# First loads in another order, an early exp at the change of layers, eps on VectorE for single tiles, and new places for the DVE units

## The chip, the cores and the metric

The kernel runs on one core of a Trainium2 chip. The core has five engines with instruction queues of their own: PE (TensorE, matrix products), ACT (ScalarE, activation functions), DVE (VectorE), POOL (GpSimd) and SP, which issues the transfers here. They meet through semaphores. Matrix products write to PSUM, eight banks of 128 x 512 floats. The metric is the device time of one launch in microseconds; the median of three runs of the kernel before is 1564.82 us (1563.92 to 1565.23).

## The reference, cut to what matters

Two pairs of layers, each an attention with one shared key and value head and then a gated MLP that mixes along the sequence; 2,048 positions, width 512, 32 heads of 16, hidden width 896 in each half:

```python
def attention(x, wq, wk, wv, wo):       # 32 query heads, one k and one v for all
    q = (x @ wq).reshape(B, S, H, Dh).transpose(0, 2, 1, 3)
    k, v = x @ wk, x @ wv
    p = softmax(einsum('bhqd,bkd->bhqk', q, k) * Dh ** -0.5)
    return einsum('bhqk,bkd->bhqd', p, v).transpose(0, 2, 1, 3).reshape(B, S, H * Dh) @ wo

def gmlp(x, w_in, w_sp, b_sp, w_out):
    z = gelu(x @ w_in)                  # tanh form
    z1, z2 = z[..., :Fh], layernorm(z[..., Fh:])
    g = einsum('ts,bsf->btf', w_sp, z2) + b_sp[None, :, None]
    return (z1 * g) @ w_out

for _ in range(2):
    x = x + attention(layernorm(x), wq, wk, wv, wo)
    x = x + gmlp(layernorm(x), w_in, w_sp, b_sp, w_out)
```

## The kernel before, in words

The program is a list of operations (`op`, `dma`, `dve`) with the tiles that they read and write, a planned duration and a priority. `_Graph.op` derives the dependencies from the keys of those tiles: an operation waits for the last writer of what it reads, and for the last writer and all readers since of what it writes. `schedule` plays the list through with planned durations and puts every engine's operations into an order by hand, as it were: whichever is ready and has the lowest priority number goes next. Where PE has too little to do, it puts in filler products (`warm`, `add_zeros`, lines 737 to 751). `emit` writes the five queues in that order, each operation with its semaphore waits. So a changed place, duration or priority can move any later instruction.

Attention is computed in groups: 32 a layer, each of 512 query columns (for the usual chunk of two tiles of 128 positions, two query columns of 256 side by side), against 16 key tiles. A unit is one group against one key tile: four blocks of 128 x 512 scores (line 925). A unit goes one of two ways.

- On ACT (`push_unit`, `push_slot`): blocks are taken two or three at a time into a slot of PSUM banks, and one activation (line 950) makes the exp of all of them and writes it to `P_ring`; then PE multiplies with V (line 969). Slots alternate between three blocks (banks 0 to 2) and two (banks 3 and 4). In a group whose bit is set in `NARROW`, both kinds have two, and bank 2 is left to side products. The planner counts 0.051 + 0.4267 us a block for an exp.
- On DVE (`push_unit_dve`): the exp is approximated with integer additions on the bits of bfloat16: four instructions of 128 x 512 (line 1003), two of 128 x 2048 (line 1012), and three PV products in place of one (line 1018).

`ON_DVE` lists for each layer and group the key tiles that go to DVE. All other work, which is called side work here, is laid between these: layer norms, keys, values, queries, the front of the MLP (`b_front`), the mixing along the sequence (`mix_stage`, `mix_late`) and the output products.

At the start, `load_x` and `load` (line 764) issue the first transfers from SP's queue, in this order: tiles 0 and 1 of X, wk, wv, wq, tiles 2 and 3 of X, then the rest. The layer norms of the first four tiles are made singly (`per_tile`): statistics on DVE (817, 818), eps added on POOL (805), the power -0.5 on POOL (807), the normalization on DVE (823), the transposition on PE (838).

At the change of layers, when the last exp of layer 0 is done, `gelu_rest` applies gelu to the rest of z2 (1272) and to z1 (1284); the last front tile brings its own gelus (1209, 1236). Then `mix_late(0, 0, ...)`, which the program lists with layer 1, adds up the mixed sums of the first two tiles (`sums_lead`, 1451), multiplies z1 by them (1459; for later tiles 1419), makes the output products (718, `w_out_r<-`), adds to X (1114), and the norms, keys and queries of layer 1 follow. The first query tile goes through ACT (`qT`, 891), and then layer 1's exps start. ACT needs another table for exp than for gelu; the table loads (ACT_TABLE_LOAD) are put in by the compiler ahead of the first activation that needs one.

After the last exp of layer 1 comes the tail: `gelu_rest` again, and `mix_late(1, ...)` for all four column blocks.

Of the kernel before, what the change touches and what calls it, by code (L numbers as in the profile page):

```python
# [8 lines left out]
I16 = mybir.dt.int16  # L9
ACTF = mybir.ActivationFunctionType  # L10
# [10 lines left out]
NF1 = 7  # L21
# [31 lines left out]
), (  # L53
# [29 lines left out]
NARROW = (4194528, 10506244)  # L83
KEEP = 6
POOL_ON = 1
POOL_XN = 0
# [42 lines left out]
class _Op:  # L129
    __slots__ = ("eng", "fn", "dur", "lat", "prio", "seq", "deps", "succ", "nleft", "chan", "chan_val",  # L130
                 "inc", "pos", "val", "clock", "t0", "task", "mode", "rows", "work", "opens", "nstart", "due", "chain", "free_lat",
                 "empties", "near_end", "heads")

    def __init__(self, eng, fn, dur, lat, prio, seq, chan, task, mode):
# [6 lines left out]
        self.heads = None  # L141
        self.opens = None
# [22 lines left out]
class _Graph:  # L165
# [3 lines left out]
    def __init__(self, nc, side, slots):  # L169
# [10 lines left out]
        self.chain = False  # L180
        self.nsem = 0
# [13 lines left out]
    def op(self, eng, fn, dur, r=(), w=(), prio=5, lat=0.0, chan=None, mode=0):  # L195
        task = next((x for x in (*w, *r) if isinstance(x, _Task)), None)
        o = _Op(eng, fn, dur, lat, prio, len(self.ops), chan, task, mode)
        o.chain = self.chain
# [34 lines left out]
    def schedule(self):  # L233
# [31 lines left out]
        slot_due = -1.0  # L265

# [73 lines left out]
        def pick(e):  # L340
# [7 lines left out]
            for ent in ready[e]:  # L348
# [6 lines left out]
                if beside(o):  # L355
                    p -= 2.0
                if best is not None and (p, o.seq) >= best[:2]:
                    continue
# [63 lines left out]
        while True:  # L422
            moved = True
            while moved:
                moved = False
                for e in ENGS:
                    if free[e]:
# [12 lines left out]
                        us = o.dur  # L440
                        if e == "pe":
# [126 lines left out]
def bass_interleave_layers__grouped_kv_mqa__mixer_gmlp__prompt_kernel(  # L568
# [43 lines left out]
    mhalf = G.sb([P, 1], FP32, "mhalf")  # L612
    mone = G.sb([P, CT], FP32, "mone")
    X = G.sb([P, NT, D], BF16, "X")
# [40 lines left out]
    ph16 = big[:].bitcast(I16)  # L655
    wspL = big[:, 4:6, :].rearrange("p a (t q) -> p a t q", q=QC)
# [72 lines left out]
    op("pool", lambda e: e.memset(mone[:], -1.0), 0.1, w=["mone"])  # L729
    op("pool", lambda e: e.memset(zeros[:], 0.0), 0.2, w=["zeros"])  # L730
# [29 lines left out]
    def load(dst, src, w, chan, kb, r=()):  # L760

        first["kb"] += kb
        first["n"] += 1
        dma(lambda e: e.dma_start(dst, src), list(r), w, chan, max(3.0, 3.2 + first["kb"] / 380.0 - 0.6 * first["n"]))

    def load_x(t0, n):
        load(X[:, t0:t0 + n, :], xsrc[:, t0:t0 + n, :], [("X", t) for t in range(t0, t0 + n)], f"x{t0}", 128 * n)
# [712 lines left out]
    for layer in range(2):  # L1480
        now["layer"] = layer
        now["group"] = 0
        for t0, n in KEYS[layer]:
# [7 lines left out]
            for si in range(NQ):  # L1491
                if sum(GROUPS[2 * si][:2]) == t0 + n:
                    q_slot(si, pr + (0.3 if si else 0.1) if layer else 3)
# [45 lines left out]
```

## Time and profile before

| | us |
|---|---|
| median of three runs (lowest to highest) | 1564.82 (1563.92 to 1565.23) |
| the profiled execution, its own time | 1566.62 |
| its span, first to last instruction | 1564.7 |
| PE busy | 1492.9 (95%) |
| ACT busy | 1484.2 (95%) |
| DVE busy | 1379.3 (88%) |
| POOL busy | 330.3 (21%) |
| exps (L950): 1289 instructions, busy | 1416.7 |
| DVE units, scores part (L1003): 980 instructions, busy | 645.0 |
| transfers, mean | 66 GB/s |

Busy time of an engine is the time in which at least one of its instructions runs; PE's contains fillers, and its products overlap. In a row of a group, the count stands behind the x, then busy microseconds and the mean nanoseconds of one; behind the second bar stands the idle time just before these instructions and what ended it. Exps overlap one another by some 0.2 us, so the mean of one is longer than the step from one to the next. A row of the timeline gives start, duration, engine, line, operation, what it writes and reads, and in brackets the idle time before it.

### The profile page before, as it was taken

The numbers are of one execution on the slowest core, as the hardware profiler recorded it, in microseconds if no ns is written. First come the engines' busy times: TensorE is split into PE (matmuls) and PEld (weight loads), VectorE is DVE, ScalarE is ACT, GpSimd is POOL, SyncE is SP. The second block draws the span as 40 slices with busy tenths as digits, with TensorE's granted clock in tenths as the row PEclk, the third lists the DMA queues.
The fourth block names the chain that finished last, engine by engine and source line by source line (L and its number), as shares of the span: only waits on it lengthen the run. The fifth ranks groups of instructions, "written<-read, shape, count | busy, mean of one in ns | idle before, by whom it ended". The sixth has DMA issues, their size and how long they took to land.

```text
span 1564.7 us, 40919 instructions
## 1 busy us (share of the span) xinstructions
PE 1492.9 (95%) x18024; PEld 487.1 (31%) x18054; DVE 1379.3 (88%) x2368; ACT 1484.2 (95%) x1336; POOL 330.3 (21%) x319
## 2 busy tenths in 40 slices
PE   8999999999999999999999999999999999999999
PEld 3222222233333233333422222323223322323343
DVE  7989999999999888886778899999899998888887
ACT  6999999999999999999799999999999999999970
POOL 2031121212221112111210025212122211212232
PEclk9999999999999999999999999999999999999999
DMA  4501010101212433545431031110121023155472
GB/s 103 136 15 15 8 26 9 22 16 39 52 35 42 98 77 116 149 109 151 114 88 21 8 78 29 21 15 15 38 59 29 22 71 90 42 153 150 109 202 68
DMA packets 186833, 103.21 MB, mean 66 GB/s; under 512 B 151072, under 2 KB 159904, under 8 KB 186656
## 3 DMA queue, kind: packets, MB, share of 16 engines
q1 hardware_dynamic: 186656, 100.60, 25.8%
q8 instruction: 141, 2.31, 0.6%
q14 instruction: 36, 0.29, 0.1%
HBM read 34.77 MB, written 29.88 MB: 41 GB/s over the span
## 4 chain that ended last, share of the span: by engine, by line
ACT 69%; PE 24%; DVE 5%; issue 1%; DMA 1%; POOL 0%; SPq 0%; DVEq 0%
ACT P_ring L950 67%; PE ps_all L713 8%; PE ps_all L925 7%; PE ps_all L969 3%; PE ps_all L718 3%; PE ps_all L1018 3%; ACT z2n L1249 1%; DVE big L1414 1%; DVE big L1003 1%; DVE X L1114 0%; DVE st L1293 0%; DVE st L817 0%; ACT L950 0%; ACT L1249 0%; DMA X<-in_A_x_dram 0%
## 5 line engine op out<-in xcount | busy, mean ns | idle before, releaser
L950 ACT ACTIVATE P_ring<-ps_all 128x1024 bf16<-128x1024 f32 (+1 forms) x1289 | 1416.7, 1313 | 18.6 <-PE ps_all L925 17.8
L1003 DVE TENSOR_SCALAR big<-ps_all 128x512 int16<-128x512 f32 x980 | 645.0, 684 | 88.9 <-PE ps_all L925 82.8
L925 PE MATMUL ps_all<-qT,kT_rep 32*128 32x512 bf16 x4096 | 602.5, 385 | 50.2 <-ACT P_ring L950 37.2
L1048 POOL TENSOR_TENSOR rden<-ot,mone 128x16 f32<-128x16 bf16 x62 | 188.0, 3033 | 776.2 <-DMA ot<-oT 775.9
L925 PEld LDWEIGHTS ps_all<-qT,kT_rep 32*128 32x128 bf16 x4096 | 154.0, 91 | 569.4 <-ACT P_ring L950 468.3
L1012 DVE TENSOR_SCALAR big<-big 128x2048 int16<-128x2048 int16 x490 | 326.5, 687 | 3.5 <-PE ps_all L1018 0.7
L969 PE MATMUL ps_all<-P_ring,V_aug 128*32 128x512 bf16 x3116 | 296.1, 387 | 3.5 <-DVE oT L1091 2.6
L1018 PE MATMUL ps_all<-big,V_ph 128*32 128x512 bf16 x2940 | 258.7, 384 | 1.2 <-DVE big L1003 0.4
L969 PEld LDWEIGHTS ps_all<-P_ring,V_aug 128*32 128x32 bf16 x3116 | 75.8, 94 | 150.8 <-issue 122.2
L1018 PEld LDWEIGHTS ps_all<-big,V_ph 128*32 128x32 bf16 x2940 | 68.5, 94 | 97.9 <-issue 59.1
L805 POOL TENSOR_SCALAR ve<-mv 128x1 f32<-128x1 f32 (+2 forms) x44 | 16.1, 365 | 377.8 <-DVE mv L818 258.7
L713 PE MATMUL ps_all<-xnTA,z2n 128*32 128x512 bf16 x1344 | 94.8, 381 | 0.0
L713 PE MATMUL ps_all<-w_in_r,xo 128*32 128x448 bf16 x960 | 62.0, 354 | 0.2 <-DVE big L1003 0.2
L1114 DVE TENSOR_TENSOR X<-ps_all,X 128x512 bf16<-128x512 f32 x64 | 43.6, 683 | 19.1 <-PE ps_all L718 15.7
L713 PE MATMUL ps_all<-xo,w_in_r 128*32 128x256 bf16 (+1 forms) x1120 | 56.5, 317 | 0.1
L718 PE MATMUL ps_all<-w_out_r,z1c 128*128 128x512 bf16 x211 | 53.5, 381 | 2.1 <-issue 0.8
L1061 POOL TENSOR_TENSOR o_norm<-ot,rden 128x128 bf16<-128x128 bf16 (+1 forms) x118 | 53.3, 471 | 4.7
L751 PE MATMUL ps_all<-ones,zeros 128*32 128x512 bf16 x632 | 54.3, 385 | 0.0
L1350 DVE TENSOR_TENSOR big<-ps_all,big 128x512 f32<-128x512 f32 x56 | 38.2, 683 | 16.5 <-PE ps_all L713 16.1
L713 PE MATMUL ps_all<-z2n 128*32 128x512 bf16 x672 | 50.0, 382 | 0.0
L713 PE MATMUL ps_all<-z1c,z2n 128*32 128x512 bf16 x672 | 49.2, 382 | 0.0
L1419 POOL TENSOR_TENSOR z1c<-big,z1c 128x512 bf16<-128x512 f32 (+1 forms) x32 | 35.0, 1104 | 63.4 <-DVE big L1414 63.3
(99 smaller groups left out, 950.0 us busy)
## 6 DMA issues: line engine op xcount, KB each, us to landing
gp_scratch<-big SPq DMA_DIRECT2D x106, 256.0 KB, 2.1
big<-gp_scratch SPq DMA_DIRECT2D x99, 256.0 KB, 3.2
out_dram<-X SPq DMA_DIRECT2D x16, 128.0 KB, 1.7
w_in_r<-in_B_w_in_dram SPq DMA_DIRECT2D x1, 1792.0 KB, 7.9
big<-gp_scratch SPq DMA_DIRECT2D x14, 128.0 KB, 2.5
X<-in_A_x_dram SPq DMA_DIRECT2D x3, 512.0 KB, 6.5
bsp<-in_B_b_sp_dram SPq DMA_DIRECT2D x8, 128.0 KB, 3.7
ot<-oT SPq DMA_TRANSPOSE x62, 2.4
```

The source lines that it names most:

```text
L713: ins = e.matmul(out_[32 * j:32 * j + 32, :], lhs[:, 32 * j:32 * j + 32], rhs, tile_position=(0, 32 * j), start=start, stop=stop)
L718: return e.matmul(out_, lhs, rhs, start=start, stop=stop)
L751: ins = e.matmul(bank32(PVB)[32 * j:32 * j + 32, :], zeros[:, 0:32], mv, tile_position=(0, 32 * j), start=False, stop=False)
L925: return e.matmul(out, kT_rep[32 * j:32 * j + 32, a, u[1] * P:(u[1] + 1) * P], qT[32 * j:32 * j + 32, q, :], tile_position=(32 * j, 0), st ...
L950: return e.activation(P_ring[:, s0:s0 + n, :], bank32(b0, n).rearrange("p (k q) -> p k q", k=n), ACTF.Exp, scale=E_SCALE)
L969: ins = e.matmul(bank32(PVB)[32 * j:32 * j + 32, :], V_aug[:, kt, :], P_ring[:, s, :], tile_position=(0, 32 * j), start=first, stop=last)
L1003: o = dve(lambda e, box=box, tk=tk: e.tensor_scalar(ph16[:, tiles[0], heads["of"][box[0]] * QC:(heads["of"][box[0]] + 1) * QC], bank32(tk. ...
L1012: dve(lambda e, a=a: e.tensor_scalar(ph16[:, tiles[a], :], ph16[:, tiles[0], :], float(PH_A[a]), None, op0=ALU.add), 0.69, base, BIG(tiles ...
L1018: ins = e.matmul(bank32(PVB)[32 * j:32 * j + 32, :], V_ph[:, a, kt, :], big[:, tiles[a], j * QC:(j + 1) * QC], tile_position=(0, 32 * j), ...
L1048: op("pool", lambda e: e.tensor_tensor(rden[:], src()[:, :, :, DH], mone[:, :, None].to_broadcast([P, CT, 4]), ALU.pow), 3.0, r=[tk, "mone ...
L1061: op("pool", lambda e, b0=b0, nb=nb, dst=dst: e.tensor_tensor(dst, src()[:, b0:b0 + nb, :, 0:DH], rden[:, b0:b0 + nb, :, None].to_broadcas ...
L1114: dve(lambda e: e.tensor_tensor(X[:, t, :], bank32(tk.bank), X[:, t, :], ALU.add), 0.69, [tk, ("X", t)], [("X", t)], prio)
```

## The change

- `ON_DVE` is replaced: in layer 0 every group keeps its number of key tiles and gets other ones; in layer 1 both change. `NARROW` of layer 1 goes from groups 2, 12, 14, 21, 23 to groups 10, 11, 15.
- The first loads: tiles 2 and 3 of X are issued behind wk, ahead of wv and wq. The planner gets fixed durations for them, and 0.5 in place of 0.7 us for issuing.
- `rstd` adds eps on DVE where it works tile by tile, and as before on POOL elsewhere.
- `gelu_rest` in layer 0 ends with an exp of a 128 x 1 tile into `early`; it is listed as a reader of all z1 tiles.
- The w_out products of `mix_late` in layer 0 are marked `calm`: their later parts keep their own priority and don't get 1.0.
- New code that the constants leave unused: key tiles whose additions go to POOL (`ON_POOL` is empty, `port`, `step2`; one memset of `step2` on POOL runs), and a raised priority for the first tiles (`LEAD` is 0).

```diff
 ON_DVE = ((
-          (6,10,14), (6,10,14), (6,10,14), (6,10,14), (2,6,9,12,14), (2,3,12,13,14), (2,4,6,11,13),
...
+          (6,10,14), (6,10,14), (6,10,14), (6,10,14), (2,3,9,10,14), (4,5,9,13,14), (2,3,10,11,14),
...
 ), (
-          (6,10,14), (6,10,14), (10,14), (14,), (6,10,14), (6,10,14), (6,10,14), (2,10,14), (2,7,8,11),
-          (6,8,10,12,14), (3,6,9,12), (3,5,8,9), (2,7,11,12,14), (2,3,9,11), (4,6,9,12), (2,4,11,12),
-          (5,6,9,13), (4,6,8,9,14), (2,5,10,12), (2,7,8,10,14), (2,4,7,14), (4,8,10,11), (3,4,6,10,14),
-          (6,9,12,14), (2,6,14), (2,3,12,13,14), (6,), (2,4,6,12,14), (6,8,13), (2,9,12), (3,10,11,13),
-          (3,8,12)
+          (6,14), (6,10,14), (10,14), (14,), (6,10,14), (2,10,14), (6,10,14), (2,6,10,14), (2,3,9,11,12),
+          (2,3,4,11), (3,6,9,11,14), (3,6,9,11,14), (2,9,11,14), (2,3,6,10,11), (3,6,12), (3,6,9,11,14),
+          (4,9,11,14), (2,4,8,12,13), (3,6,10,11), (3,7,11,14), (2,3,7,13), (4,9,11,12,13), (3,5,7,11),
+          (3,7,8,9,14), (6,10), (2,3,10,13), (5,10,13), (2,6,12,14), (3,6,11,13), (4,9,12), (5,10,11,13),
+          (9,11,12)
 ))
...
-NARROW = (4194528, 10506244)
+NARROW = (4194528, 35840)
...
+    op("pool", lambda e: e.memset(step2[:], (PH_A[2] - PH_A[1]) * 65537), 0.1, w=["step2"])
...
-    load_x(0, 2)
-    load(wk_nat[:], A_wk.rearrange("(kd p) r -> p kd r", p=P), ["wk_nat"], "wk", 16)
-    load(wv_nat[:], A_wv.rearrange("(kd p) r -> p kd r", p=P), ["wv"], "wv", 16)
-    load(wq_r[:], A_wq.rearrange("(kd p) n -> p kd n", p=P), ["wq"], "wq", 512)
-    load_x(2, 2)
+    load_x(0, 2, 2.9)
+    load(wk_nat[:], A_wk.rearrange("(kd p) r -> p kd r", p=P), ["wk_nat"], "wk", 16, 3.0)
+    load_x(2, 2, 4.0)
+    load(wv_nat[:], A_wv.rearrange("(kd p) r -> p kd r", p=P), ["wv"], "wv", 16, 4.0)
+    load(wq_r[:], A_wq.rearrange("(kd p) n -> p kd n", p=P), ["wq"], "wq", 512, 5.0)
...
         for a, b in ([(i, i + 1) for i in range(i0, i0 + ni)] if per_tile else [(i0, i0 + ni)]):
-            op("pool", lambda e, a=a, b=b: e.tensor_scalar(ve[:, a:b], mv[:, a:b, 1], LN_EPS, None, op0=ALU.add),
-               0.25, r=[("mv" + n, i) for i in range(a, b)], w=[("ve" + n, i) for i in range(a, b)], prio=prio)
+            if per_tile:
+                dve(lambda e, a=a, b=b: e.tensor_scalar(ve[:, a:b], mv[:, a:b, 1], LN_EPS, None, op0=ALU.add), 0.15,
+                    [("mv" + n, i) for i in range(a, b)], [("ve" + n, i) for i in range(a, b)], prio)
+            else:
+                op("pool", lambda e, a=a, b=b: e.tensor_scalar(ve[:, a:b], mv[:, a:b, 1], LN_EPS, None, op0=ALU.add),
+                   0.25, r=[("mv" + n, i) for i in range(a, b)], w=[("ve" + n, i) for i in range(a, b)], prio=prio)
...
+        allk = []
         for t0, n in Z1_LATE:
             k = [("z1", f, t) for f in range(NF1) for t in range(t0, t0 + n)]
...
+            allk += k
+        if not now["layer"]:
+            op("act", lambda e: e.activation(early[:], mhalf[:], ACTF.Exp), 1.5, r=allk + [("z1", f, NT - 1) for f in range(NF1)] + ["mhalf"],
+               w=["early"], prio=5)
...
         for t in range(t0, t0 + n):
-            tk = _Task()
+            tk = _Task(calm=layer == 0 and CALM)
             products(tk, NF1, lambda e, ft, t=t, tk=tk: mm1(
                 e, bank32(tk.bank), z1c[:, ft, t * P:(t + 1) * P], w_out_r[:, ft, :], ft == 0, ft == NF1 - 1),
                 lambda ft: [("z1", ft, t), "w_out"], chain)
```

More of the change, by code (lines that the diff above doesn't have):

```diff
@@ L141, in __init__ @@
         self.heads = None
+        self.port = 0
         self.opens = None
@@ L180, in __init__ @@
         self.chain = False
+        self.lead = False
         self.nsem = 0
@@ L197, in op @@
         o = _Op(eng, fn, dur, lat, prio, len(self.ops), chan, task, mode)
-        o.chain = self.chain
+        o.chain = self.chain or self.lead
         if task is not None:
@@ L356, in pick @@
                     p -= 2.0
+                if o.port == 1 and now < long_till:
+                    p += PORT_LATE
+                if o.port == 2 and quick_till > now:
+                    continue
                 if best is not None and (p, o.seq) >= best[:2]:
@@ L440, in schedule @@
                         us = o.dur
+                        if o.port == 2:
+                            long_till = now + us
+                        elif o.port:
+                            if now < long_till:
+                                us += min(2 * (long_till - now) / 3, 1.2)
+                            quick_till = now + us
                         if e == "pe":
@@ L989, in push_unit_dve @@
         hg, kt, first, last = u[:4]
+        on_pool = ON_POOL[now["layer"]] and kt in ON_POOL[now["layer"]][now["gi"]]
         assert not first and not last
@@ L1456, in lead @@
                    prio=pr, lat=PE_LAT)
[L1457 to L1460 removed]
+            parts = [(t, t + 1) for t in range(n)] if LEAD > 1 else [(0, n)]
+            for a, b in parts:
+                z = z1c[:, f0:f0 + nf, a * P:b * P]
+                zk = [("z1", ft, t) for ft in fs for t in range(a, b)]
+                dve(lambda e, z=z, a=a, b=b: e.tensor_tensor(
+                    z, all_sums().rearrange("p (a q) -> p a q", q=w)[:, :, a * P:b * P], z, ALU.mult),
+                    0.15 + 0.135 * nf * (b - a), [tk] + zk, zk, chain + 0.01 * a)
         for f0 in range(0, NF1, m):
```

45 lines of the change are left out of this document (29 added, 16 removed), and 8 rows, old and new, of the table ON_DVE.

## The prediction

> **What bounds the kernel now.** I read the page's busy table first, then the waits of ACT, then busy time by stretch, and last the timeline around the two places where ACT stands still. The groups (with forms kept apart) and the waits of ScalarE:
>
> ```profile
> L950 ACT ACTIVATE P_ring<-ps_all 128x1536 bf16<-128x1536 f32 x538 | 837.6, 1557 | 6.1 <-PE ps_all L925 5.7
> L950 ACT ACTIVATE P_ring<-ps_all 128x1024 bf16<-128x1024 f32 x751 | 807.8, 1138 | 12.5 <-PE ps_all L925 12.1
> ```
> ```profile
> ACT P_ring L950 <- PE ps_all L925: 17.8, 11, 11.9
> ACT qT L891 <- PE ps_all L718: 9.7, 1, 9.7
> ```
>
> The second number of a wait is how often, the third the longest. One exp wait is the 11.9 us before the first exp, one wait is the 9.7 us at the change of layers; the other ten exp waits are 5.9 us together in 1,480 us. So ACT's exp stream sets the time: a start of 13.9 us, layer 0, the change, layer 1 to 1,496.7, then a tail of 68.0 us that PE and DVE share. A microsecond of exp work or of either standstill is a microsecond of the end. The stretches (columns: PE, weight load, DVE, ACT, POOL, granted clock, DMA share, GB/s) show how close the others are:
>
> ```profile
> 0.00:14.00 14.00, 10.45 (x113) 5.61 (x113) 9.88 (x29) 1.40 (x2) 6.97 (x27) 1.00 0.65 191
> 14.00:24.00 10.00, 9.43 (x116) 3.66 (x112) 7.83 (x20) 8.26 (x8) 1.28 (x2) 0.66 0.03 7
> 900.00:1100.00 200.00, 186.63 (x2382) 58.45 (x2379) 186.47 (x316) 199.08 (x180) 57.12 (x46) 0.99 0.16 31
> 1100.00:1300.00 200.00, 194.84 (x2382) 58.30 (x2379) 185.97 (x311) 199.70 (x188) 40.02 (x33) 1.00 0.17 44
> 1497.00:1565.00 68.00, 63.24 (x416) 28.09 (x410) 54.30 (x88) 17.33 (x16) 24.09 (x26) 1.00 0.46 132
> ```
>
> ACT is at 99.7% from 900 to 1300, but DVE there is already at 93%: 27.6 us idle in 400. The timeline at the start and at the change:
>
> ```profile
> 2.83 2.16 SPq L764 DMA_DIRECT2D X<-in_A_x_dram  x4
> 3.45 1.29 DVE L817 BATCH_NORM_STATS2 st<-X 128x6 f32<-128x512 bf16 x2 [0.62 <-DMA X<-in_A_x_dram]
> ...
> 7.41 0.69 DVE L817 BATCH_NORM_STATS2 st<-X 128x6 f32<-128x512 bf16 x1 [1.18 <-DMA X<-in_A_x_dram]
> 8.02 0.40 DVE L823 TENSOR_SCALAR xn<-X,mv,rs 128x512 bf16<-128x512 bf16 x1
> ```
> ```profile
> 746.20 2.53 ACT L1284 ACTIVATE z1c<-z1c 128x1792 bf16<-128x1792 bf16 x2
> 746.76 2.22 DVE L1459 TENSOR_TENSOR z1c<-ps_all,z1c 128x512 bf16<-128x512 f32 x4 [0.49 <-PE ps_all L1451]
> 749.26 2.97 PE L718 MATMUL ps_all<-w_out_r,z1c 128*128 128x512 bf16 x13
> 758.43 0.60 ACT L891 ACTIVATE qT<-ps_all 128x512 bf16<-128x512 f32 x1 [9.70 <-PE ps_all L718]
> 759.04 1.28 ACT L950 ACT_TABLE_LOAD   x1
> 760.34 10.60 ACT L950 ACTIVATE P_ring<-ps_all 128x1024 bf16<-128x1024 f32 x10
> ```
>
> At the start, DVE waits 1.18 us for the third tile of X while the finished statistics of the second wait behind it. At the change, the last gelu ends at 748.73, and the products z1*g (L1459), which the chain runs through, begin 2 us before that.
>
> **The change part by part.**
>
> *New places.* Layer 0 keeps its number of DVE units in every group, so its exp work is unchanged. Layer 1 goes from 117 to 119 units (two more, both among groups 8 to 21; groups 22 to 31 keep 36) and from five narrow groups to three. Stepping through the slot rule gives 714 two-block and 560 three-block exps for 751 and 538: 8 blocks and 15 instructions fewer. The kernel prices an exp at 0.051 + 0.4267 per block; all 1289 exps and 3116 blocks come to 1395 by that, against 1416.7 us on the page with the stalls in it, so it is close. Then -15 x 0.051 - 8 x 0.4267 = -4.2 us. With the difference of the two rows (0.419 a block) and the whole rest of 1416.7 spread over the instructions (0.086 each) it is -4.6. I take -4.2, since stalls need not fall with the count. For this DVE gets 2 x (4 x 0.684 + 2 x 0.687) = 8.2 us more, from the rows of L1003 and L1012, inside the 27.6 us idle; without that cover it would be +8.2 on the path. PE gets eight more PV matmuls a unit and more single score matmuls, some 2 us, hidden by its waits for ACT (14 to 17 us in every 50). What the other places do to the small stalls I can't read: I take 0. The stalls are 21 us in all (1416.7 - 1395), so a gain above some 4 is unlikely; and 4 lost would be four more like the longest exp wait in mid-stream, 1.28 us at 552.
>
> *First loads.* X's tiles 2 and 3 leave the queue third instead of fifth, at about 1.74 instead of 2.83. Alone in the queue X's first load took 2.7 us to its first use, so the third tile is there near 4.5 to 5, ahead of DVE. The wait of 1.18 goes; the second xn moves from 8.02 to about 6.6, and its transposes, kT and the first exp with it: -1.4. wv and wq are issued 0.5 us later; wq took 4.4 us to land, so about 7.2 to 7.8 with 256 KB now ahead of it, and its matmuls, at 10.52 before, would come near 9.1: still covered, with little over a microsecond. What is late next is DVE, which does statistics and kT in one queue. Ends: 0, if DVE's order eats it, and -2.5, if kT also no longer waits behind the statistics at 10.16.
>
> *The early exp.* It reads every z1 tile, and it is put into the program ahead of the layer-1 products that overwrite z1. So the dependency tracker makes each of them wait for it. L1459 then waits for: last gelu 748.73, table load 1.29, a 128x1 exp (the 128x384 and 128x512 activations took 0.48 and 0.60, which leaves about 0.15 to 0.2 for one element), the semaphore: about 750.25 instead of 746.76, +3.5. Behind L1459 in DVE's queue stand X's addition and the statistics of layer 1's first tiles, and PE waits for it with w_out (749.26, 0.28 after L1459's last), so the whole chain to qT moves by that. Back comes the load at 759.04: without it exp starts when the first scores are there, 759.38 plus 0.43 (the step from 13.45 to 13.88 at the start), 759.8 for 760.34: -0.5. The row of the wait gives the bounds: 0 if the products were late anyway, +3.6 if nothing overlaps.
>
> A page of the Trainium skill weighs on this. "ScalarE: Activation LUTs", section "What ACT_TABLE_LOAD costs", puts a switch of sets at about 2.66 us, load plus drain. Here the load at 730.10 is followed by a gelu at 731.39, 1.29 later, so this trace does not bear it out; so it gets no chance of its own. By the page the step would cost 1.4 more and the sum would be 1562.3.
>
> *eps on VectorE.* For single tiles 20 POOL instructions (128x1, 248 ns mean) become DVE ones. POOL's way from statistics to power is 0.40 us (752.39 to 752.79); on DVE a small instruction takes between 0.06 (the 128x1 memset) and 0.17 (aggregate), then a hop of 0.1. Saved: 0.1 to 0.25 each, where it lies on a chain: in the last front tile, whose gelus end ACT's run (-0.3, since that POOL eps took 0.39), at layer 1's second tile (-0.25), once in the tail (-0.2); at the start it is within the -1.4. DVE's 20 instructions are at most 3.4 us over the span, beside other work.
>
> *The rest at nothing.* One POOL memset of 0.10 us ahead of the ones delays only the first warming matmuls. The port, lead and POOL-unit code is switched off by its constants. The w_out products of layer 0 lose their raised priority once begun: an order between 761 and 900, where ACT waits little; within +-0.5. There the late start also lets the mixing work run ahead, and the gaps at 773, 899, 939 and 942 (0.49, 0.34, 0.51, 0.29) may shrink: -0.5.
>
> Sum: -4.2 - 1.4 + 3.5 - 0.5 - 0.3 - 0.25 - 0.2 - 0.5 = -3.9 (rounded). The span was 1564.7, and the profiled execution took 1566.62, 1.9 around the span and 1.8 above the median of the three runs, 1564.82. I take the difference off the median: 1560.9.
>
> **The rivals.** *More is gained.* The products' wait for the early exp costs nothing, because the products come later in the new order, or the stalls fall by as much: -3.9 - 3.5 = -7.4, 1557.4. Against it: L1459 follows its sums by 0.1 us and ACT is busy from 731 to 748.7 almost without a gap.
>
> *Two small gains fail.* DVE's order eats the earlier load and the gaps after 761 stay: -3.9 + 1.9 = -2.0, 1562.8, no measurable change. For it: between 10.2 and 13.4 DVE has no idle time before qT.
>
> *Slower: DVE becomes the bound between 900 and 1300.* It is at 93% and takes 8.2 us more in a stretch that should be 4.2 shorter: 380.6 of 396, 96%. If its idle 27.6 us is all waits for PE that no order removes, the stretch grows by 8.2 instead of shrinking by 4.2: 12.4 worse, 1573.3. It decides from 7 us lost, that is when more than half of the added DVE work shows. Against it: ACT does not wait for DVE units itself, only through PE's order and banks, and the listed exp waits on DVE are none.
>
> *The clock.* From 14 to 24 us the granted clock is 0.66 on average, and the first eight exps, 13.88 to 23.4, take about 2 us more than at full pace. "TensorE: Matmul & The Clock Gate" in the Trainium skill says the window that decides this is free-running (section "What's actually happening"); three runs cannot show that. An earlier start may keep or lose these 2 us: in the range.
>
> **How the numbers follow.** A change below 0.2%, 3.1 us, can't be told from none. The forecast, 0.50, own range 1558 to 1563.5, about two thirds of it faster by over 3.1 us. More is gained, 0.18: faster. Gains fail, 0.16: same. Slower, 0.16. So faster 0.33 + 0.18 = 0.51, same 0.17 + 0.16 = 0.33, slower 0.16. The range to 8 in 10 runs from 1556, leaving out the rare lower end of the second case, to 1567, with the lower part of the slow one.
>
> **What would show it.** 714 and 560 exps in the rows of L950; no wait of DVE for X near 7 us and the first exp near 12.5 (13.88); a table load near 748.7, L1459 waiting for ACT until about 750.3, and between last gelu and first exp of layer 1 some 14 us instead of 11.6, with no load behind the qT copy. DVE above 95% in the middle of layer 1, with ACT gaps named after PE scores, would show the slow case. The prediction is wrong if the first exp of layer 1 is not delayed, if exp stalls change by over 4 us, or if the tail of 68 us moves by more than 1.

## The result, and the profile after

The changed kernel takes 1562.47 us (median; 1559.05 to 1564.86), the kernel before in the same comparison 1565.23 us (1563.46 to 1567.0): a ratio of 0.9981, 95% interval 0.9975 to 0.9987, so 2.0 to 3.9 us faster. The medians differ by 2.8 us where the forecast was 3.9. That lies inside the stated range, but the time itself is nearer to 1562.8, the rival in which two small gains fail, than to the forecast of 1560.9. Several terms of the sum were further off than the sum. The profiled executions took 1566.62 and 1562.47 us, with spans of 1564.7 and 1560.2.

ScalarE's groups with forms kept apart, after:

```profile
L978 ACT ACTIVATE P_ring<-ps_all 128x1536 bf16<-128x1536 f32 x560 | 874.7, 1562 | 3.6 <-PE ps_all L953 3.3
L978 ACT ACTIVATE P_ring<-ps_all 128x1024 bf16<-128x1024 f32 x714 | 780.5, 1143 | 12.5 <-PE ps_all L953 12.3
```

Its waits, after (first how long in all, then how often, then the longest):

```profile
ACT P_ring L978 <- PE ps_all L953: 15.7, 9, 11.3
ACT qT L919 <- PE ps_all L740: 11.1, 1, 11.1
```

ACT is still the stream that everything hangs on: 1274 exps for 1289, 11.3 us before the first, 11.1 at the change of layers, and 4.4 us in the other eight waits. Where the stages end is read from the first exp of each layer and from the table loads that the compiler puts behind a layer's last exp. Before:

```profile
730.10 1.28 ACT L1272 ACT_TABLE_LOAD   x1
...
1496.75 1.28 ACT L1272 ACT_TABLE_LOAD   x1
```

After:

```profile
13.30 3.29 ACT L978 ACTIVATE P_ring<-ps_all 128x1024 bf16<-128x1024 f32 x3 [11.29 <-PE ps_all L953]
...
727.69 1.28 ACT L1306 ACT_TABLE_LOAD   x1
...
747.03 0.20 ACT L1324 ACTIVATE early<-mhalf 128x1 f32<-128x1 f32 x1
...
758.35 0.60 ACT L919 ACTIVATE qT<-ps_all 128x512 bf16<-128x512 f32 x1 [11.12 <-PE ps_all L740]
...
759.60 1.02 ACT L978 ACTIVATE P_ring<-ps_all 128x1024 bf16<-128x1024 f32 x1 [0.66 <-PE ps_all L953]
...
1489.53 1.28 ACT L1306 ACT_TABLE_LOAD   x1
```

| stage | before | after | difference | forecast |
|---|---|---|---|---|
| to the first exp | 13.9 | 13.3 | -0.6 | -1.4 |
| exps of layer 0 | 716.2 | 714.4 | -1.8 | 0 |
| change of layers, to the next exp | 30.2 | 31.9 | +1.7 | +2.4 |
| exps of layer 1 | 736.4 | 729.9 | -6.5 | -4.7 |
| tail, last exp to end | 68.0 | 70.7 | +2.7 | -0.2 |
| sum | 1564.7 | 1560.2 | -4.5 | -3.9 |

These are single executions. About 1 us of the 4.5 is clock: the mean granted clock of the two was 0.997 and 0.998 (see below).

Busy time by stretch, after, in the columns of before:

```profile
0.00:14.00 14.00, 9.80 (x113) 5.40 (x113) 10.50 (x33) 1.99 (x2) 5.86 (x24) 1.00 0.64 191
14.00:24.00 10.00, 9.37 (x131) 3.84 (x128) 9.06 (x23) 9.13 (x9) 1.28 (x2) 0.83 0.02 4
759.60:1489.53 729.93, 699.05 (x8490) 219.87 (x8509) 652.14 (x1108) 727.73 (x648) 146.55 (x127) 1.00 0.24 58
900.00:1100.00 200.00, 190.16 (x2373) 58.15 (x2366) 191.56 (x320) 199.18 (x183) 57.63 (x46) 0.99 0.16 29
1100.00:1300.00 200.00, 194.31 (x2441) 59.81 (x2440) 186.94 (x316) 199.97 (x180) 36.96 (x33) 1.00 0.17 43
1497.00:1565.00 68.00, 58.24 (x363) 26.05 (x356) 48.22 (x79) 10.24 (x10) 23.14 (x21) 0.99 0.39 122
```

The exps of layer 1 before, in the same columns:

```profile
760.30:1496.75 736.45, 706.08 (x8519) 220.49 (x8539) 647.53 (x1097) 733.44 (x665) 150.43 (x129) 1.00 0.24 60
```

DVE rose from 372.4 to 378.5 us of the 400 between 900 and 1300, and ACT did not slow down for it. In layer 1's stretch ACT stood idle for 3.0 us before and 2.2 us after; the rest of the 6.5 us is busy time.

**How runs are compared below.** Every run has a span and a mean granted clock of PE, and within a kernel the span follows the clock. The changed kernel has 1557.3 and 1557.7 us at 1.000, 1558.1 to 1559.3 at 0.999, and 1561.7 to 1562.8 at 0.996. A straight line through all kernels, with one slope and a height for each, falls by 1.13 us for each 0.001 of clock. Its height at 1.000 is given as "at full clock"; it is a span, some 2 us below the time of its run, and stands with the standard error of the mean. It is 1561.38 (+-0.06) before and 1557.86 (+-0.14) after, a difference of 3.5 us. The experiments were run in four batches on three chips, each with the kernel before beside it, and its own height differs between them: 1561.1 on chip 7, 1561.5 on chip 1, 1561.3 and 1561.7 on chip 2. So a difference of half a microsecond between kernels of different batches is not shown, whatever the standard errors say.

A second means: the planner reorders everything when one duration changes. So several experiments keep the planned order of every engine, and change after planning only what is named ("order kept").

### The profile page after: what moved, and what is told of

It is laid out like the page before. It is cut to its first block, busy times and chain, and to the rows that moved or that the text cites. A ratio compares the mean times of both kernels' runs of the same rounds, so it can differ in the third digit from the quotient of the medians.

```text
span 1560.2 us, 40997 instructions
## 1 busy us (share of the span) xinstructions
PE 1486.9 (95%) x18067; PEld 488.8 (31%) x18094; DVE 1386.4 (89%) x2392; ACT 1478.8 (95%) x1322; POOL 324.1 (21%) x308
## 4 chain that ended last, share of the span: by engine, by line
ACT 84%; PE 9%; DVE 4%; DMA 1%; issue 1%; SPq 0%; POOL 0%; DVEq 0%
ACT P_ring L978 82%; PE ps_all L740 3%; PE ps_all L735 2%; PE ps_all L953 2%; ACT z2n L1283 1%; PE ps_all L997 1%; DVE big L1032 1%; PE ps_all L1052 1%; DVE big L1453 1%; DVE big L1046 0%; DMA X<-in_A_x_dram 0%; DVE st L845 0%; DVE st L1332 0%; DVE X L1148 0%; DMA big<-gp_scratch 0%
## 5 line engine op out<-in xcount | busy, mean ns | idle before, releaser
L978 ACT ACTIVATE P_ring<-ps_all 128x1536 bf16<-128x1536 f32 (+1 forms) x1274 | 1411.0, 1327 | 16.0 <-PE ps_all L953 15.7
L1032 DVE TENSOR_SCALAR big<-ps_all 128x512 int16<-128x512 f32 x988 | 650.1, 685 | 78.1 <-PE ps_all L953 70.5
L1046 DVE TENSOR_SCALAR big<-big 128x2048 int16<-128x2048 int16 x494 | 331.2, 690 | 4.7 <-PE ps_all L1052 2.0
L997 PE MATMUL ps_all<-P_ring,V_aug 128*32 128x512 bf16 x3108 | 292.6, 387 | 3.0 <-DVE oT L1125 1.9
L1052 PEld LDWEIGHTS ps_all<-big,V_ph 128*32 128x32 bf16 x2964 | 69.6, 94 | 99.3 <-issue 57.6
L833 POOL TENSOR_SCALAR ve<-mv 128x4 f32<-128x4 f32 (+2 forms) x32 | 10.8, 339 | 335.4 <-DVE mv L846 219.0
L774 PE MATMUL ps_all<-ones,zeros 128*32 128x512 bf16 x676 | 58.5, 388 | 0.0
```

What stands on the lines that cost most here:

```text
L774: ins = e.matmul(bank32(PVB)[32 * j:32 * j + 32, :], zeros[:, 0:32], mv, tile_position=(0, 32 * j), start=False, stop=False)
L978: return e.activation(P_ring[:, s0:s0 + n, :], bank32(b0, n).rearrange("p (k q) -> p k q", k=n), ACTF.Exp, scale=E_SCALE)
L997: ins = e.matmul(bank32(PVB)[32 * j:32 * j + 32, :], V_aug[:, kt, :], P_ring[:, s, :], tile_position=(0, 32 * j), start=first, stop=last)
L1032: o = dve(lambda e, box=box, tk=tk: e.tensor_scalar(ph16[:, tiles[0], heads["of"][box[0]] * QC:(heads["of"][box[0]] + 1) * QC], bank32(tk. ...
L1046: dve(lambda e, a=a: e.tensor_scalar(ph16[:, tiles[a], :], ph16[:, tiles[0], :], float(PH_A[a]), None, op0=ALU.add), 0.69, base, BIG(tiles ...
L1052: ins = e.matmul(bank32(PVB)[32 * j:32 * j + 32, :], V_ph[:, a, kt, :], big[:, tiles[a], j * QC:(j + 1) * QC], tile_position=(0, 32 * j), ...
```

## Experiments: the early exp and the change of layers

*The early exp left out, order kept.*

```diff
         order = self.schedule()
+        x = self.early_op
+        order["act"].remove(x)
+        self.ops.remove(x)
+        for o in self.ops:
+            o.deps.pop(x, None)
```

> The changed kernel with every engine's order kept, and only the early exp and the waits for it gone. Theory (the products' wait for the early exp delays the whole chain at the change of layers): the products z1*g start 3 us or more earlier against the last exp of layer 0 (16.7 us after it, as in the kernel before, in place of 20.0); the table load is back behind the qT copy; first exp of layer 1 at 29.5 to 30.5 us after the last of layer 0 in place of 31.9; the whole 1.5 to 2.5 us faster than the changed kernel. Rival (the wait only uses time in which the chain would stand anyway, and the load saved pays for it): first exp of layer 1 within 0.5 us of the changed kernel's or later, time the same within 0.7 us.

*Kept, but no longer waited for, order kept.*

```diff
         order = self.schedule()
+        for o in self.ops:
+            o.deps.pop(self.early_op, None)
```

> The changed kernel with every engine's order kept and the early exp kept, but nothing waits for it any more (it writes and reads no tile of theirs). Theory: both gains together, products as early as without the early exp and no table load between the qT copy and the first exp: first exp 0.5 us earlier than without the early exp, 29.0 to 30.0 us after the last exp of layer 0; the whole 2 to 3 us faster than the changed kernel. Rival (the load is hidden either way): the same as without the early exp within 0.2 us at the first exp.

Measured: 1561.4 us, ratio to before 0.9979 (0.997 to 0.9987), without the early exp, and 1560.56, 0.9972 (0.9963 to 0.9981), without the waits; at full clock 1557.04 (+-0.29) and 1557.13 (+-0.24), 0.8 and 0.7 under the changed kernel. Both ran on chip 7, where the kernel before is lower too: against it they gain 4.1 and 4.0 us, and the changed kernel, in the one batch in which it was run beside these, on chip 2, 3.9. So no gain at the end is shown. From the last exp of layer 0 to the next exp it is 32.6 us without the early exp and 31.9 without the waits. The timeline without the early exp:

```profile
746.22 1.30 DVE L1458 TENSOR_TENSOR big<-ps_all,big 128x256 f32<-128x256 f32 x3 [2.11 <-PE ps_all L745]
747.43 2.21 DVE L1505 TENSOR_TENSOR z1c<-ps_all,z1c 128x512 bf16<-128x512 f32 x4
758.70 1.28 ACT L983 ACT_TABLE_LOAD   x1
```

Nothing holds the products z1*g (L1505) any more, and they still start 20 us after the last exp: in DVE's queue three additions stand ahead of them, which wait for PE. So on the chip the products' wait for the early exp costs next to nothing. The theory, as it was written, falls, and the rival holds. What the early table load is worth can be read here: 32.6 less 31.9, 0.65 us at the first exp, as the second expectation had it, and nothing that shows at the end.

*Planned anew, with an early exp that reads no z1 tile.* It waits for the gelus alone, through keys of their own; places and narrow groups are chosen anew.

```diff
-               w=k, prio=0.5 if t0 < CT else 4)
+               w=k + [("gelu", t0)], prio=0.5 if t0 < CT else 4)
             us = 0.0
-            allk += k
+            allk.append(("gelu", t0))
...
-            op("act", ..., 1.5, r=allk + [("z1", f, NT - 1) for f in range(NF1)] + ["mhalf"],
+            op("act", ..., 1.5, r=allk + ["gelu_fine", "mhalf"],
```

> The changed kernel, planned anew, with an early exp that waits for the gelus alone and that no product waits for; the places are chosen anew for that plan, not as long as those of the changed kernel, so its whole is expected some us slower than the changed kernel and is not the question. Theory (the reads of z1 put the products, and with them all of the change of layers, later in the plan): first exp of layer 1 at 28.5 to 30.5 us after the last of layer 0 in place of 31.9, with no table load behind the qT copy and z1*g from about 16.7 us after the last exp instead of 20. Rival (the change is as long because DVE and PE have that much to do): 31.4 us or more.

Measured: 1569.26 us, ratio 1.0025 (1.0015 to 1.0035), and the change of layers as follows:

```profile
728.50 1.28 ACT L1292 ACT_TABLE_LOAD   x1
...
748.27 0.20 ACT L1310 ACTIVATE early<-mhalf 128x1 f32<-128x1 f32 x1
...
757.83 4.71 ACT L964 ACTIVATE P_ring<-ps_all 128x1024 bf16<-128x1024 f32 x4 [0.78 <-PE ps_all L939]
```
```profile
744.83 2.22 DVE L1486 TENSOR_TENSOR z1c<-ps_all,z1c 128x512 bf16<-128x512 f32 x4 [0.49 <-PE ps_all L1476]
```

The products start 16.3 us after the last exp, and the first exp comes 29.3 us after it instead of 31.9, as the theory had it. So the plan decides. With the reads of z1 the planner sees that the products must wait, and puts other work ahead of them on DVE and PE; taking the wait away afterwards does not bring another order. But the 2.6 us are not those of the reads alone, since this version has other places too. The next run keeps the places.

*Only the change of layers planned anew.* A second plan without the waits, in which from 5 planned us after the first exp of layer 1 every engine follows the order of the first.

```diff
+        self.deps0 = {o: dict(o.deps) for o in self.ops}
+        self.first = self.schedule()
+        self.again(757.0)         # drops the waits; follows self.first for work planned after 757
         order = self.schedule()
```

> The changed kernel with the early exp kept, nothing waiting for it, the change of layers planned anew, and from about 5 us after the first exp of layer 1 on every engine's order as in the changed kernel. Theory (layer 1 is one stream of exps, so an earlier first exp moves the end by as much): first exp 29.0 to 29.8 us after the last of layer 0 in place of 31.9, layer 1's stream as long as before, the whole 2 to 3 us faster than the changed kernel. Rival (the mixing of layer 0's late tiles, which runs beside the first exps of layer 1, is what the stream waits for next): first exp as early, but layer 1's stream 1.5 to 2.5 us longer and the whole within 1 us of the changed kernel.

Beside it on the same chip, the changed kernel once more:

> The changed kernel itself, unaltered, beside the run above on the same chip: 1560.5 to 1563 us, 0.9975 to 0.9987 of the kernel before; the tail of its profile 69.5 to 70.7 us, and the half-clock windows at some of the places seen so far.

Measured: 1561.66 us, ratio 0.997 (0.9958 to 0.9983), beside 1560.51, 0.9966 (0.9953 to 0.9979), for the changed kernel itself; at full clock 1558.32 (+-0.26), against 1557.86 for all runs of the changed kernel. The first exp came 30.7 us after the last one, 1.2 earlier than in the changed kernel, and layer 1's exps took 733.0 us instead of 729.9. Some of that lies in two clock windows at 863 us, and most here:

```profile
765.67 3.08 PE L767 MATMUL ps_all<-big,z2n 128*128 128x512 bf16 x12
...
768.69 0.39 PE L980 MATMUL ps_all<-qT,kT_rep 32*128 32x512 bf16 x3
...
769.13 2.37 ACT L1005 ACTIVATE P_ring<-ps_all 128x1536 bf16<-128x1536 f32 x2 [2.32 <-PE ps_all L980]
```

The next thing that the exps wait for is the mixing of layer 0's late tiles, twelve products in a row in PE's queue ahead of the scores. An earlier first exp waits there, in the order that this version was made to follow. The rival holds as to the end: no gain over the changed kernel. The first exp moved only half as far as both expected.

The versions side by side, counted from the last exp of layer 0 (the start of the table load behind it):

| early exp | places | order | z1*g starts | first exp |
|---|---|---|---|---|
| none (before) | old | own plan | 16.7 | 30.2 |
| none | new | own plan (the second run of the next section) | 18.0 | 31.6 |
| waited for (the changed kernel) | new | own plan | 20.0 | 31.9 |
| left out | new | of the changed kernel | 20.0 | 32.6 |
| not waited for | new | of the changed kernel | 20.0 | 31.9 |
| not waited for | new | change of layers planned anew | 17.8 | 30.7 |
| reads no z1 | chosen anew | own plan | 16.3 | 29.3 |

At least two things lengthen the change. With the same places, the waits in the plan cost 1.2 us at the first exp (31.9, in all five profiles of that order with the early exp, for 30.7). And the new places cost 1.4 by themselves: the kernel before with the new places and no early exp has this:

```profile
726.47 1.28 ACT L1272 ACT_TABLE_LOAD   x1
...
744.45 2.22 DVE L1459 TENSOR_TENSOR z1c<-ps_all,z1c 128x512 bf16<-128x512 f32 x4 [1.12 <-PE ps_all L1451]
...
758.06 2.37 ACT L950 ACTIVATE P_ring<-ps_all 128x1024 bf16<-128x1024 f32 x2
```

With 0.65 back for the early load and 0.2 for eps (below), that makes the +1.7 of the changed kernel. Each of the four was taken in a plan of its own, so the fit is no proof.

## Experiments: places, loads, eps

*Old places in the new kernel*, planned anew: `ON_DVE` and `NARROW` of before.

```diff
-NARROW = (4194528, 35840)
+NARROW = (4194528, 10506244)
...
 ON_DVE = ((                       # here cut: all 64 groups as in the kernel before
```

> The changed kernel with the places of the DVE units and the narrow groups of before. Theory (the places shorten layer 1's exp stream by 4.2 us of work and some 2 of stalls, and the tail gives 2.7 back): layer 1's stream 734 to 738 us instead of 729.9, tail 67 to 69 us instead of 70.7; the whole 2.5 to 5 us slower than the changed kernel, so slower than the kernel before by about 0 to 2. Rival (the gain comes from the loads and the eps, and the places move nothing): within 1 us of the changed kernel.

*New places in the old kernel*, the other way round.

> The kernel before with the new places and narrow groups alone. Theory (places and plan belong together; the new places bring their 4.2 us of exp work only in the order they were chosen for, as the old places lost 36 us in the new order): 10 us or more slower than the kernel before, with exp waits of several us at a few points of layer 1 or layer 0. Rival (the new places are better by themselves): 2 to 4 us faster than the kernel before, exp stream of layer 1 729 to 732 us.

Measured: 1598.85 us, ratio 1.0214 (1.0201 to 1.0227), and 1588.63 us, 1.0149 (1.0135 to 1.0163). Each set of places lost in the other's plan. Layer 1's exps take 771.3 us with the old places in the new kernel. The largest two of ACT's waits, 13.9 and 9.0 us, make up most of the loss; this is the first, after a look at what PE does meanwhile:

```profile
1372.84 2.76 PE L735 MATMUL ps_all<-z1c,z2n 128*32 128x512 bf16 x48
...
1375.43 2.55 PE L774 MATMUL ps_all<-ones,zeros 128*32 128x512 bf16 x44
...
1379.58 1.78 DVE L1340 TENSOR_SCALAR z2n<-z2n,mv,rs 128x896 bf16<-128x896 bf16 x4
...
1380.57 0.62 PE L735 MATMUL ps_all<-xnTA,z2n 128*32 128x512 bf16 x8 [2.09 <-DVE z2n L1340]
...
1384.60 1.45 ACT L978 ACTIVATE P_ring<-ps_all 128x1536 bf16<-128x1536 f32 x1 [13.94 <-PE ps_all L953]
```

PE runs mixing and 44 fillers, and then waits for DVE's normalization, while no scores are issued for 11 us: none stand there in PE's queue, which is the plan's order. Both expectations of the first run missed by 30 us. In the second run layer 1's exps take 747.9 us instead of 736.4 and the tail 79.2 instead of 68.0; its theory held as to the time, but no exp wait inside a layer is longer than 2.4 us.

*First loads as before*, once planned anew and once with the order kept.

```diff
         order = self.schedule()
+        first = order["sp"][:5]
+        order["sp"][:5] = [first[0], first[1], first[3], first[4], first[2]]
```

> The changed kernel with the first loads issued and planned as before. Theory (the load order is worth what the first exp shows): first exp at 13.6 to 14.2 us instead of 13.3, the whole 0.4 to 1.5 us slower. Rival (the start is also where the granted clock drops, and the order decides how long): the first 24 us lose up to 2 us more than the first exp shows, and the whole is 1.5 to 3 us slower.

> The changed kernel with every engine's order kept; only SP issues wv and wq ahead of tiles 2 and 3 of X again. Theory (the third tile's arrival sets the start): VectorE waits for it 1.5 to 2.2 us more at 5.4, the first exp comes at 14.5 to 15.5 instead of 13.3 and the whole is 1 to 2 us slower than the changed kernel. Rival (what comes before the first exp is given back in layer 0 or in the tail, as the run with the old loads and a new plan hints: first exp 1.05 later, whole not slower): within 0.7 us of the changed kernel.

Measured: planned anew 1560.74 us, ratio 0.9976 (0.9968 to 0.9985), first exp at 14.35, 1557.43 (+-0.27) at full clock; with the order kept 1563.34, 0.9988 (0.9979 to 0.9997), first exp at 14.04, 1558.72 (+-0.32). VectorE, with the order kept:

```profile
7.55 0.69 DVE L847 BATCH_NORM_STATS2 st<-X 128x6 f32<-128x512 bf16 x1 [2.17 <-DMA X<-in_A_x_dram]
8.16 0.72 DVE L853 TENSOR_SCALAR xn<-X,mv,rs 128x512 bf16<-128x512 bf16 x2
```

In one order the loads are worth 0.86 us at full clock (two standard errors above nothing) and 0.74 at the first exp; profiles in the changed kernel's order with the new loads have the first exp anywhere from 13.0 to 13.5. Planned anew, the old loads give a first exp 1.05 later and no loss that can be seen; both expectations of that run had a loss and missed. With the order kept, the wait of 2.2 us came as expected; the first exp was 0.5 earlier than the theory had it, and the loss lies between theory and rival.

*eps back on POOL, order kept*: the additions that the change took to DVE move to POOL's queue, each just ahead of its power. They are twelve and not twenty: the profile after has 12 of one column on DVE and 8 still on POOL, where a norm of one tile is not made in the tile-by-tile way.

```diff
         order = self.schedule()
+        for x in self.eps:
+            y = next(o for o, k in x.succ if o.eng == "pool")
+            order["dve"].remove(x)
+            order["pool"].insert(order["pool"].index(y), x)
+            x.eng = "pool"
...
```

> The changed kernel with every engine's order kept; only the twenty single-tile eps additions stand in POOL's queue again, just ahead of their power. Theory: each costs its chain 0.1 to 0.3 us; first exp 0.1 to 0.4 later, the change of layers 0.3 to 0.7 longer (32.2 to 32.6 us), the whole 0.4 to 1.2 us slower. Rival (VectorE's twenty extra instructions cost there what the chain saves): within 0.3 us.

Measured: 1563.21 us, ratio 0.9981 (0.9972 to 0.999); at full clock 1557.82 (+-0.21), 0.04 under the changed kernel. The change of layers is 0.2 longer, and nothing of it shows at the end. The rival holds.

## Experiments: the tail and the clock

*Half the products of layer 1's second mixing stage left out, order kept.*

```diff
-            def mk(e, s, ft=ft, tk=tk):
+            def mk(e, s, ft=ft, tk=tk, half=now["layer"] and st):
+                if half and s % 2:
+                    return half_of[0]
...
```

> The changed kernel with every engine's order kept; in the second mixing stage of layer 1 every other product is left out, so that sum lacks half its terms. 188 of these products stand behind the last exp, 132 in the kernel before; half of 188 is 5.1 us of PE at 0.217 for four. Theory (PE's unfinished mixing is what lengthened the tail): the tail falls from 70.7 to between 65.5 and 69 us, the last exp stays within 1.5 us, the whole is 2 to 5 us faster. Rival (the tail is set by the chain of the last front tile, the gelus and the fetched sums, and the products only fill holes): tail within 0.7 us of 70.7.

Measured: 1561.49 us, ratio 0.9976 (0.9966 to 0.9987), where the changed kernel has 0.9981 (0.9975 to 0.9987). At full clock it is 1556.01 (+-0.29), 1.9 under the changed kernel, but here the line cannot be trusted: the mean clock of its runs is 0.9966, against 0.9980, and the half-clock window in its tail cost nothing, as is shown below. The last exp is where it was (1489.2), and the tail 69.6 us in place of 70.7. The first stretch of the tail, without the products:

```profile
1489.20:1504.00 14.80, 12.00 (x129) 5.28 (x122) 12.76 (x32) 14.66 (x13) 3.17 (x8) 0.88 0.95 257
```

And the changed kernel:

```profile
1489.50:1504.00 14.50, 14.07 (x207) 6.55 (x198) 12.70 (x32) 14.32 (x14) 3.01 (x8) 1.00 1.01 232
```

PE lost over a third of its products there, and nothing got shorter: they fill holes in the chain of the last front tile. (PE, with less to do, also got a half-clock window at 1494.) Before, the last of these products ended at 1510.6, in the holes; in the changed kernel 48 are left for the middle of the tail, 2.8 us in which PE does nothing else:

```profile
1512.69 1.29 DVE L1453 TENSOR_TENSOR big<-ps_all,big 128x512 f32<-128x512 f32 x2 [1.04 <-DMA big<-gp_scratch]
...
1534.66 2.77 PE L735 MATMUL ps_all<-xnTA,z2n 128*32 128x512 bf16 x48
1537.59 9.01 PE L740 MATMUL ps_all<-w_out_r,z1c 128*128 128x512 bf16 x41 [0.16 <-issue]
```

The same place without half of the products:

```profile
1533.57 0.83 PE L735 MATMUL ps_all<-xnTA,z2n 128*32 128x512 bf16 x12
1534.73 0.83 PE L735 MATMUL ps_all<-xnTA,z2n 128*32 128x512 bf16 x12 [0.33 <-DVE big L1458]
1536.16 9.01 PE L740 MATMUL ps_all<-w_out_r,z1c 128*128 128x512 bf16 x41 [0.60 <-DVE big L1394]
```

And with all of them, in the version without the early exp, whose tail is 69.8 us:

```profile
1532.19 2.77 PE L740 MATMUL ps_all<-xnTA,z2n 128*32 128x512 bf16 x48
1535.12 9.01 PE L745 MATMUL ps_all<-w_out_r,z1c 128*128 128x512 bf16 x41 [0.16 <-issue]
```

Count from the end of the last exp: 1489.53 in the changed kernel, 1489.22 with half of the products, 1487.88 without the early exp. The 48 products begin 45.1, 44.4 and 44.3 us later, and the w_out products behind them 48.06, 46.94 and 47.24 us later. So the window at 1494 cost nothing, and half of the products gone is worth 0.3 us: what PE saves, it mostly waits for DVE. The other 0.8 us, between the changed kernel and both others, goes with the wait of 1.04 us for a fetched sum. Only the two profiles of the changed kernel have that wait, with tails of 70.7 and 70.5 us; the five versions in its order that lack it have 69.6 to 70.1.

The expected 65.5 to 69 us was missed, and the rival's 70 to 71.4 narrowly; its reading, that the products fill holes, is the nearer one. Of the 2.7 us that the tail grew, some 0.8 go with the fetched sum. The cause of the other 1.9 stays open. PE is busy 65.4 us there for 63.5, with 192 of these products for 140, but leaving half of them out gave little of it back.

*Fillers issued twice, order kept.*

```diff
-    G.warm = warm
+    G.warm = lambda e, b, mode: (warm(e, b, mode), warm(e, b, mode))[1]
...
-    G.zeros = add_zeros
+    G.zeros = lambda e, mode: (add_zeros(e, mode), add_zeros(e, mode))[1]
```

> The changed kernel with every engine's order kept; every filler product of PE is issued twice. The profiles so far each have one to three windows of 3.4 us (or 6.8) at half the granted clock, at places that come back (16, 59, 860 to 903, 937 to 983, 1312, 1356 us), and the spans of the changed kernel go from 1557.3 at a mean clock of 1.000 to 1562.8 at 0.996. Theory (PE's work is just short of what holds the clock at these places, and the windows make the spread): with more filler the mean clock is 0.999 to 1.000 and the median 1558.5 to 1560.5, 2 to 4 us under the changed kernel. Rival (the windows come from something else, or the fillers hold up scores as much as they save): clock as before, time the same within 1 us or slower.

Measured: 1583.31 us, ratio 1.0115 (1.0098 to 1.0132). The profiled execution had no half-clock window within its work, mean clock 1.000, and still a span of 1579.7: 922 more filler products stand in PE's queue. Of four runs two still had a mean clock of 0.998, and the changed kernel too has runs at 1.000, so these four don't show whether more filler holds the clock. Filler in bulk costs some 22 us at full clock, much more than the 2 to 4 us that it could save. The rival holds as to the time.

## Why the prediction was right, and where its steps were not

By its own signs it was wrong in one place: the tail of 68 us moved by 2.7 us in the profiles, and more than 1 was to count against it. The exp stalls moved by 4.1 (8.3 us less in the two exp stages, for 4.2 less work), at its limit of 4; part of that is clock.

- *New places.* The counts came as worked out: 714 and 560 exps, for which the prediction took -4.2 us. Layer 1's stream fell by 6.5, so 2.3 more, of which 0.5 had been put down to the gaps after 761. ACT's idle time in that stretch gives 0.8 of the 2.3; the other 1.5 is busy time, and no run says whether it was stalls inside the exps or too low a price for an exp. That the places could be priced by themselves was luck: the runs with one set of places in the other's plan lost 36 and 23 us. The step that failed is the bound on what other places can cost, which was taken from the stalls before; a plan that doesn't fit them has waits of 14 us.
- *First loads.* The wait for the third tile went, the second xn came when it should (both were done by 6.9), but of 1.4 us only 0.6 arrived at the first exp (0.8 in the changed kernel's second profile). The step that failed is DVE as what "is late next", taken at no cost. PE was done with kT's products at 8.93, but DVE's order puts the statistics of the fifth tile ahead of kT's copy and waits for that tile:

```profile
8.32 0.61 PE L882 MATMUL ps_all<-xnTA,wk_rep 128*128 128x256 bf16 x4 [0.63 <-DVE xnTA L869]
...
9.50 0.70 DVE L845 BATCH_NORM_STATS2 st<-X 128x6 f32<-128x512 bf16 x1 [1.11 <-DMA X<-in_A_x_dram]
...
10.77 0.86 DVE L886 TENSOR_SCALAR kT_rep<-ps_all,rows 128x256 bf16<-128x256 f32 x2
```

- *The early exp.* The products started 20.0 us after the last exp instead of 16.7, as forecast (+3.3 for +3.5), and the first exp came 1.7 later; from the last gelu to the first exp it is 13.9 us, for some 14. That the number came out is luck in part: the step that failed is the cause. With the order kept, the products don't move when the wait goes; the waits act through the plan, with 1.2 us at the first exp, and the new places by themselves add 1.4, which the prediction put at nothing. The price at the end isn't borne out either: "a microsecond of either standstill is a microsecond of the end" failed in the one version with an earlier first exp in the same places, whose stream waited for mixing at 769 instead. What the early exp costs at the end is 0.8 us by the heights at full clock and 0.2 with each version taken against the kernel before of its own batch, so nothing clear.
- *eps.* Put at -0.75 in three places; it is worth nothing that can be measured (-0.04 +-0.25). Twelve instructions went to DVE, not the twenty that the prediction counted.
- *Layer 0.* Put at 0, it gave 1.8 us in the profiles. From 14 to 24 us ACT was busy 9.13 instead of 8.26, with half the clock lost for 3.4 us instead of 6.8; that is chance as far as it is clock. In the changed kernel's second profile, with no such window in layer 0, the stage took 713.2 us, 1.2 less than with one. So one window fewer can be most of the 1.8.
- *The tail.* Put at -0.2, it was +2.7. The step that failed is that the tail was priced as if it began with the same work left over: PE's added work was counted as hidden in its waits for ACT, and that the exps end 7 us sooner leaves more side work behind them was not asked. 52 more mixing products did stand there. But what they cost is small as far as it was tried; 0.8 us go with a fetched sum that comes late, and the rest is open.
- *The rivals.* DVE was not the bound from 900 to 1300: 94.6% busy, with ACT at 99.8%. Two smaller gains did fail, eps and more than half of the loads; the second rival had named the loads and the gaps after 761. The stalls of layer 1 and layer 0 made up for them. That the sum came out close is luck: errors of +2.9 (tail) and +0.8 (loads) stood against -1.8 (layer 0), -1.8 (layer 1) and -0.7 (change) in the profiles.

The `calm` mark of the w_out products was not taken back in any run by itself, nor were the planner's new durations for the first loads in the order kept; what they do in the plan is not known.

None of the versions run is clearly better than the changed kernel: without the waits for the early exp, 0.9972 (0.9963 to 0.9981) against 0.9981 (0.9975 to 0.9987), 0.7 us at full clock, and 0.1 with each taken against the kernel before of its own batch.

## What to carry to other kernels

In a kernel whose order is planned as a whole, an edit acts first on the plan. Undo a part with the order kept and with the order planned anew; here the two answers differed, and together they told the wait from the order. Keep everything else the same, the places too, or the plan answers for both. A gain ahead of the engine that sets the time is a gain at the end only if nothing else stands in its way shortly after. Work that filled holes beside a stream is left over when the stream gets shorter; whether it costs anything there has to be read from the waits, not from its busy time.

## What the runs showed of the hardware

The half-clock windows are 3.4 us long, or 6.8, and differ between executions of one program. Profiles of versions with the same order have them at 16 us or at 59, at 860, 900 or 980. The last products of a profile don't count; within the work there were one to four in those profiles (one of 6.8 us counted as two), and none in the one with doubled fillers. One window of 3.4 us lowers the mean clock of a run of 1,560 us by 0.0011, which by the line costs about 1.2 us; the one in the tail without half of the products cost nothing. That explains most of the spread of 5.8 us between runs of the changed kernel: the standard deviation is 1.6 us, and 0.7 about the line. The Trainium skill ("TensorE: Matmul & The Clock Gate", section "What's actually happening") calls the window free-running and 3413 ns long. The records agree in length. That it is free-running no run here shows; the moving places only fit with it.
